# LSH attention and two MLP stages on one core: score pieces of 384 columns, another order of the attention, and one small addition moved to VectorE

## The chip, the cores and the metric

The kernel runs on one core of a Trainium2 chip. The metric is device time in microseconds of one execution. The core has TensorE (PE, matmuls, results in PSUM), VectorE (DVE), ScalarE (ACT), GpSimd (POOL) and SyncE (SP, which issues the DMAs); PEld in a profile is TensorE's loading of weights.

## The reference

The first part is attention over 2 batches and 8 heads, 768 positions of 64 dimensions. Queries and keys are hashed to 6 bits each, by the signs of their products with a random projection; a query attends only to the keys of its own bucket:

```python
mask = q_bucket[:, :, :, None] == k_bucket[:, :, None, :]
scores = scale * np.matmul(q, k.transpose(0, 1, 3, 2))
scores = np.where(mask, scores, -1000000000.0)
scores = scores - np.max(scores, axis=-1, keepdims=True)
attn = np.exp(scores)
attn = attn / (np.sum(attn, axis=-1, keepdims=True) + 1e-09)
return np.matmul(attn, v).astype(np.float32)
```

Its output, 1536 tokens of 512, goes through an MLP, `((x @ w1) * (x @ w2)) @ w3 @ w_out`, and that through a mixture of four experts, `out += p[e] * (relu(x @ e1[e]) @ e2[e])`.

## The kernel before

Every float32 matmul is made of products of parts: a value is split into a high part, rounded to the type that PE takes, and the low rest, and three of the four products are summed. Hence the many pairs "hi" (an ACT copy, or POOL's) and "lo" (a subtraction on DVE or POOL).

The attention works on 48 units (16 heads x 3 blocks of 256 queries). For each unit `unit(u)` records:

- S (two, of 128 queries each): the score matmuls into a tile `s_ps` of two PSUM banks, 768 key columns in the pieces `SEG` (512 and 256 columns). The sign bits of the hash ride along as extra rows (`kb`, `lo`), so that scores of other buckets become huge.
- mx (DVE, line 436): copies the score tile to `e` and takes its minimum per row (scores are negated).
- ex (ACT, line 439): the exponential in place, with the row sums in columns 6 and 7 of the small tile `sm`.
- r1 (POOL, line 452): adds 1e-9 to the two sums; r2 (DVE, line 454): the reciprocal of both.
- en (POOL, line 449, every fourth on ACT, line 448): normalizes `e` by it.
- T (PE, line 470): transposes of `e` into `t_ps`; hi (ACT, line 476) and lo (DVE, line 478) split them into `et`.
- pv (PE): products with the values into `pv_ps`; po (ACT, lines 496 and 503) and xa (DVE, line 498; from unit 27 on POOL, line 506, behind a DMA pm) sum the two halves into the MLP's input `xa`.

Per head, `head` records loads on the SP queue, splitting on POOL (lines 360, 167, 170) and copies by DMA; per two heads, `pair` records the sign bits: matmuls `bits_of`, in the same pieces `SEG`, the comparison `is_pos` on DVE (line 386) and DMA copies. `first_head` does it for head 0 alone, with the queries' comparison in two parts of 256 and 512 columns.

Beside the attention run the first 8 weight conversions (`conv64`, n from 0 to 7): each loads half a tile of 64-bit weights and turns it to high and low parts, with the DVE operations c0, c1, c2, c3 and cd (lines 207, 209, 212, 215, 220), two ACT operations and two POOL operations (lines 170 and 223). When `xa` of the first 512 tokens is there and their weights are converted, PE has 96 "fill" matmuls (fm) of the first MLP stage for times when it has no attention work (into `t_ps[2]`, which is free for them from unit 38 on, and `s_ps`). The rest of the MLP (`u_ps`, `o_ps`) begins when all attention work has ended.

The order of the work on all engines is written out by a planner, `emit_all`. Each operation is recorded by `op` with an engine, a duration in ns (fixed by hand), what it depends on, and a priority: its time T in units of P = 5500 plus P times the `RANK` of its group. The planner goes through the recorded durations, and on each engine takes the ready operation of the lowest priority value; the instructions are then issued in that order on each engine's queue. The ranks of the eight conversions are `C0 + n * CP`. So a changed duration or rank changes the order on every engine, PE and SP included, while what is computed stays.

Of the kernel before, what the change touches and what calls it, by code (L numbers as in the profile page):

```python
# [14 lines left out]
ALU = mybir.AluOpType  # L15
# [9 lines left out]
RANK = {
    "C0": 16.68,
    "CP": 16.1,
    "S0": -239.52,
    "S1": 27.05,
    "T0": -88.98,  # L30
    "T1": -71.39,
    "T2": -86.81,
    "b0": -70.87,
    "b1": -163.79,
    "bits": -188.45,
    "en": -138.6,
    "ex0": 12.29,
    "ex1": -50.98,
    "fd": -30.85,
    "fx": -49.15,  # L40
    "hi0": -17.87,
    "hi1": -151.69,
    "hi2": -87.16,
    "ld": -138.95,
    "lo0": -71.6,
    "lo1": -482.92,
    "lo2": -138.58,
    "lv": -106.52,
    "mx0": -542.16,
    "mx1": -84.39,  # L50
    "p0": -19.19,
    "p1": -131.31,
    "pm": -135.95,
    "po": -194.17,
    "pr2": -131.6,
    "prep": 2.16,
    "pv": 12.21,
    "r1": -72.77,
    "r2": -255.45,
    "v": 13.17,  # L60
    "xa": -226.06,
    "xb": -108.68,
}
GROUP = {
    **dict.fromkeys(("sc", "h", "l", "k1", "k2", "k3", "dq"), "prep"),
# [9 lines left out]
def tile_lsh_attention_moe(ctx, tc, qk, v, projc, w1, w2, w3T, w_out, dp, e1, e2, out):  # L75
    nc = tc.nc
    B, H, D2, S = qk.shape
# [33 lines left out]
    xa = const.tile([128, TT, DM], F32, name="xa")  # L111
# [6 lines left out]
    PC = projc.shape[1] - 1  # L118
# [3 lines left out]
    XP = 27  # L122
# [22 lines left out]
    sm_t = tiles(6, [128, 8], "sm")  # L145
    ap.tile([128, APAD], F32, name="apad")
    s_ps = tiles(2, [128, 1024], "s_ps", p=pp)
    SEG = (slice(0, 512), slice(512, S))
    pv_ps = pp.tile([128, 512], F32, name="pv_ps")[:, 0:256]
    t_ps = tiles(3, [128, 512], "t_ps", p=pp)  # L150
    f_ps = t_ps[2]
# [2 lines left out]
    def mm(o, l, r, start, stop):  # L154
        nc.tensor.matmul(out=o, lhsT=l, rhs=r, start=start, stop=stop)  # L155
# [30 lines left out]
    def conv64(n, dst, half, src):  # L186
        r = raws[n % NRAW]

        def hi_():
            return slots[dst][:, 0, half * 512:(half + 1) * 512]  # L190

        def lo_():
            return slots[dst][:, 1, half * 512:(half + 1) * 512]

        ri = r.bitcast(I32)
        lw, hw = (ri.rearrange("p (a b) -> p a b", b=2)[:, :, i] for i in range(2))
        c, t = cbuf[:, n % NCB, 0], cbuf[:, n % NCB, 1]
# [27 lines left out]

    P = 5500.0
# [21 lines left out]
    def op(key, eng, dur, fn, deps, prio, group=None):  # L248
        keys[key] = len(ops)
        group = group or group_of(key)  # L250
        ops.append((eng, dur, fn, deps, prio + P * RANK.get(group, 0.0), group))
# [122 lines left out]
        op(("vl", hh), "POOL", 956, lambda: pool_lo(vv[:, :, D:2 * D], rv, vv[:, :, 0:D]), [("vh", hh)], Tv)  # L374

    def bits_of(ps, hs):
        for r in SEG:
            for i, hh in enumerate(hs):
                a = hh % 2
                hi, lo = hh_t[hh % HR], ll_t[hh % HR]  # L380
                mm(ps[:, r], pbh[:, a, :], hi[:, r], i == 0, False)
                mm(ps[:, r], pbl[:, a, :], hi[:, r], False, False)
                mm(ps[:, r], pbh[:, a, :], lo[:, r], False, i == len(hs) - 1)

    def is_pos(dst, ps, r, c=slice(0, S)):
        nc.vector.tensor_scalar(out=dst, in0=ps[r, c], scalar1=thr[r], scalar2=amp[r], op0=ALU.is_gt, op1=ALU.mult)  # L386

    def first_head():
        ps, free_, n = take_s()
        lo, kb = ll_t[0], kb_t[0]  # L390
        q, k = slice(0, PC), slice(64, 64 + PC)
        T = -1e6
        op(("bm", -1), "PE", 970, lambda: bits_of(ps, (0,)), [("h", 0), ("l", 0), ("pb", 0)] + free_, T, "b0")
        op(("mk", 0), "DVE", 930, lambda: is_pos(kb[k], ps, k), [("bm", -1)], T, "b0")
        for i, (key, c) in enumerate(((("mq", 0), slice(0, 256)), (("sf", n), slice(256, S)))):
            op(key, "DVE", (330, 600)[i], lambda c=c: is_pos(lo[64:64 + PC, c], ps, q, c), [("mk", 0)], T + i, "b0")

    def pair(p):
        T = (2 * p - 1.6) * 3 * P
# [14 lines left out]
    def unit(u):  # L414
# [30 lines left out]
        def norm(t):  # L445
# [698 lines left out]
```

## Time and profile before

| | |
|---|---|
| median of 3 runs | 983.35 us (982.66 to 983.57) |
| the profiled execution, from first to last instruction (span) | 980.4 us; the page gives no other time of it |
| instructions | 14358 |
| PE busy | 966.2 us, 99% |
| PEld busy | 833.1 us, 85% |
| DVE busy | 718.6 us, 73% |
| ACT busy | 455.8 us, 46% |
| POOL busy | 200.4 us, 20%, all of it in the first 264 us |
| TensorE's granted clock | 1.00 throughout |

Busy shares are means over the whole span. The attention lies in about the first 264 us, the MLP stages behind it; the shares of the two parts differ much, so the views by stretch are the ones to read. A PE that counts as busy is not PE at its peak, since matmuls are pipelined and their ends are modelled. A time in brackets after an instruction is idle time of its engine ahead of it, with what ended it.

### The profile page before, as it was taken

How to read it: one execution, taken by the hardware profiler on the slowest of the kernel's cores; microseconds unless marked ns; L12 is line 12 of the kernel's file. 1: busy time of each engine (PE TensorE's matmuls, PEld its weight loads, DVE VectorE, ACT ScalarE, POOL GpSimd, SP SyncE). 2: the span in 40 equal slices, each digit the busy share in tenths (PEclk: the TensorE clock that was granted, in tenths of full speed). 3: DMA queues.
4: the chain of work that ended last, by engine and by line, in shares of the span. 5: the costliest groups of instructions: out<-in, count | busy, mean ns of one | idle time of the engine just before them, and what ended most of it. 6: DMA issues, size and time to landing. Idle time of an engine off the chain costs nothing.

```text
span 980.4 us, 14358 instructions
## 1 busy us (share of the span) xinstructions
PE 966.2 (99%) x5227; PEld 833.1 (85%) x5227; DVE 718.6 (73%) x1401; ACT 455.8 (46%) x864; POOL 200.4 (20%) x244
## 2 busy tenths in 40 slices
PE   8999999999999999999999999999999999999998
PEld 7999989888888888888888888888888888888886
DVE  7999999998599974964798745777457674476543
ACT  6999999987443422444543223322232322323121
POOL 6978878886100000000000000000000000000000
PEclk9999999999999999999999999999999999999999
DMA  6645444330133331330021102001021000200011
GB/s 171 184 124 137 114 105 116 90 92 12 54 126 113 127 108 43 110 106 1 22 65 44 44 1 84 25 22 35 9 75 34 22 24 21 64 22 1 1 65 66
DMA packets 42728, 65.58 MB, mean 67 GB/s; under 512 B 5752, under 2 KB 25784, under 8 KB 42656
## 3 DMA queue, kind: packets, MB, share of 16 engines
q1 hardware_dynamic: 42512, 64.65, 22.3%
q8 instruction: 41, 0.67, 0.3%
q14 instruction: 31, 0.25, 0.1%
q10 hardware_dynamic: 144, 0.01, 0.0%
HBM read 47.22 MB, written 3.15 MB: 51 GB/s over the span
## 4 chain that ended last, share of the span: by engine, by line
PE 86%; DVE 9%; POOL 2%; issue 1%; ACT 1%; DMA 0%; DVEq 0%; POOLq 0%; ACTq 0%
PE u_ps L155 50%; PE o_ps L155 22%; PE s_ps L155 5%; PE pv_ps L155 4%; PE t_ps L470 4%; DVE et L478 3%; DVE e L436 3%; PE t_ps L155 1%; PE t_ps L534 1%; DVE cbuf L215 0%; POOL e L449 0%; DVE xa L498 0%; DVE bt L386 0%; DVE cbuf L207 0%; ACT et L476 0%
## 5 line engine op out<-in xcount | busy, mean ns | idle before, releaser
L155 PE MATMUL o_ps<-slotl,hl 128*128 128x512 f32 x768 | 180.0, 390 | 0.0
L155 PEld LDWEIGHTS o_ps<-slotl,hl 128*128 128x128 f32 x768 | 142.9, 188 | 28.9
L155 PE MATMUL u_ps<-xh,slotl 128*128 128x512 f32 (+1 forms) x672 | 137.2, 359 | 0.0
L155 PEld LDWEIGHTS u_ps<-xh,slotl 128*128 128x128 f32 x672 | 114.3, 189 | 18.7
L155 PE MATMUL u_ps<-xh,slot 128*128 128x512 f32 (+1 forms) x576 | 116.8, 353 | 0.0
L155 PEld LDWEIGHTS u_ps<-xh,slot 128*128 128x128 f32 x576 | 97.8, 189 | 16.6
L951 DVE TENSOR_TENSOR m<-m,u_ps 128x512 f32<-128x512 f32 x96 | 63.2, 682 | 62.1 <-PE u_ps L155 60.8
L478 DVE TENSOR_TENSOR et<-t_ps,et 128x512 fp32r<-128x512 f32 x144 | 96.4, 680 | 4.8 <-ACT et L476 4.3
L439 ACT ACTIVATE e<-e,sm 128x768 f32<-128x768 f32 x96 | 89.8, 938 | 10.4 <-DVE e L436 9.7
L436 DVE TENSOR_SCALAR_CACHE_REDUCE e<-s_ps 128x768 f32<-128x768 f32 x96 | 90.4, 945 | 2.1 <-PE t_ps L470 1.0
L155 PE MATMUL pv_ps<-et,vv 128*128 128x256 f32 x576 | 89.3, 294 | 0.9 <-DVE xa L498 0.4
L470 PE MATMUL t_ps<-ident,e 128*128 128x128 f32 x576 | 84.2, 274 | 4.3 <-DVE et L478 3.9
L155 PE MATMUL u_ps<-slotl,hl 128*128 128x512 f32 x384 | 87.7, 389 | 0.0
L476 ACT ACTIVATE et<-t_ps 128x512 fp32r<-128x512 f32 x144 | 82.1, 595 | 9.9 <-PE t_ps L470 5.8
L155 PEld LDWEIGHTS u_ps<-slotl,hl 128*128 128x128 f32 x384 | 72.1, 188 | 15.0
L470 PEld LDWEIGHTS t_ps<-ident,e 128*128 128x128 f32 x576 | 66.0, 140 | 13.2 <-DVE et L478 5.6
L155 PEld LDWEIGHTS pv_ps<-et,vv 128*128 128x128 f32 x576 | 74.3, 190 | 2.0 <-DVE xa L498 0.6
L449 POOL TENSOR_SCALAR e<-e,sm 128x768 f32<-128x768 f32 x72 | 65.9, 922 | 8.1 <-DVE sm L454 5.7
L946 DVE SCALAR_TENSOR_TENSOR hl<-gl,hl 128x512 fp32r<-128x512 f32 x32 | 22.1, 692 | 47.7 <-ACT hl L1088 47.7
L943 ACT ACTIVATE hl<-m 128x512 fp32r<-128x512 f32 x32 | 20.3, 633 | 76.6 <-DVE m L951 76.6
L161 ACT ACTIVATE m<-u_ps 128x512 f32<-128x512 f32 x32 | 19.1, 598 | 79.0 <-issue 61.9
L155 PE MATMUL s_ps<-ka,hh 128*128 128x512 f32 x192 | 52.8, 356 | 3.1 <-DVE e L436 2.5
(157 smaller groups left out, 1563.0 us busy)
## 6 DMA issues: line engine op xcount, KB each, us to landing
wraw<-in_e SPq DMA_DIRECT2D x64, 256.0 KB
wraw<-in_w SPq DMA_DIRECT2D x16, 512.0 KB
wraw<-in_w3T SPq DMA_DIRECT2D x16, 512.0 KB
r<-in_qk SPq DMA_DIRECT2D x15, 384.0 KB
wraw<-in_w_out SPq DMA_DIRECT2D x8, 512.0 KB
rv<-in_v SPq DMA_DIRECT2D x16, 192.0 KB
ka<-hh SPq DMA_DIRECT2D x15, 192.0 KB
kb<-hh SPq DMA_DIRECT2D x15, 192.0 KB
```

Source lines behind the costliest of these rows:

```text
L155: nc.tensor.matmul(out=o, lhsT=l, rhs=r, start=start, stop=stop)
L161: nc.scalar.activation(out=dst, in_=ps, func=AF.Copy)
L436: op(("mx", u, t), "DVE", 873, lambda ps=ps, m=m, e=e: nc.vector.tensor_scalar(out=e, in0=ps[:, 0:S], scalar1=THR, scalar2=None, op0=ALU.m ...
L439: op(("ex", u, t), "ACT", 921, lambda e=e, m=m, rs=rs: nc.scalar.activation(out=e, in_=e, func=AF.Exp, scale=-1.0, bias=m, accum_out=rs), ...
L449: return "POOL", 872, lambda: nc.gpsimd.tensor_scalar(out=e, in0=e, scalar1=r[:, t:t + 1], scalar2=1.0, op0=ALU.mult, op1=ALU.mult)
L470: nc.tensor.transpose(out=ps[:, k, t * 128:(t + 1) * 128], in_=e_t[2 * (u % ER) + t][:, kt * 128:(kt + 1) * 128], identity=ident)
L476: op(("hi", n), "ACT", 480, lambda ps=ps, et=et: nc.scalar.activation(out=et[:, 0], in_=ps, func=AF.Copy), [("T", u, j), ("pv", n - NET)], Tj)
L478: op(("lo", n), "DVE", 602, lambda ps=ps, et=et: nc.vector.tensor_tensor(out=et[:, 1], in0=ps, in1=f(et[:, 0]), op=ALU.subtract), [("hi", ...
L534: nc.tensor.transpose(out=t_ps[i % 2][:, 0:128], in_=ident, identity=ident)
L943: op(key, "ACT", 480, lambda: nc.scalar.activation(out=hl_t[n % 2][:, 0], in_=m_t[m], func=AF.Relu), after, clock[0])
L946: op(key, "DVE", 602, lambda: nc.vector.scalar_tensor_tensor(out=hl_t[n % 2][:, 1], in0=src(), scalar=0.0, in1=f(hl_t[n % 2][:, 0]), op0=A ...
L951: nc.vector.tensor_tensor(out=out, in0=a, in1=b, op=o)
```

## The change

Four things are done.

- `SEG` now holds pairs of a place in PSUM and a range of columns: the score tile's 768 columns lie as 384 in the first 512 of the tile and 384 in the second 512. Score and sign matmuls are 384 columns each. `row` and `cols` let DVE read such a tile as two runs of 384. The first head's comparison is two parts of 384.
- r1 is recorded on DVE, as the same tensor_scalar on the same two columns, with 75 ns in place of 295 for the planner.
- The planner's durations for the first eight conversions' DVE operations, for S and for pv are other numbers.
- `RANK` is another table, and each of the eight conversions has a rank of its own (cv0 to cv7) in place of `C0 + n * CP`.

```diff
-    SEG = (slice(0, 512), slice(512, S))
+    SEG = ((slice(0, 384), slice(0, 384)), (slice(512, 896), slice(384, S)))
+
+    def row(ps, r=slice(0, 128)):
+        return ps[r].rearrange("p (a b) -> p a b", a=2)[:, :, 0:384]
+
+    def cols(x):
+        return x.rearrange("p (a b) -> p a b", a=2)
...
-        slow = (400, 700, 2700) if beside else (335, 602, 1460)
+        slow = (616, 750, 2700, 365, 792) if beside else (335, 602, 1460, 335, 335)
...
-            ("DVE", slow[0], [("c0", n)], "c1",
+            ("DVE", slow[3], [("c0", n)], "c1",
...
-            ("DVE", slow[0], [("c2", n)], "c3",
+            ("DVE", slow[4], [("c2", n)], "c3",
...
-        for i, (key, c) in enumerate(((("mq", 0), slice(0, 256)), (("sf", n), slice(256, S)))):
-            op(key, "DVE", (330, 600)[i], lambda c=c: is_pos(lo[64:64 + PC, c], ps, q, c), [("mk", 0)], T + i, "b0")
+        for i, (key, c) in enumerate(((("mq", 0), SEG[0]), (("sf", n), SEG[1]))):
+            op(key, "DVE", 470, lambda c=c: is_pos(lo[64:64 + PC], ps, q, c), [("mk", 0)], T + i, "b0")
...
-                for c in SEG:
-                    mm(ps[:, c], hi[:, r], ka[:, c], True, False)
-                for c in SEG:
-                    mm(ps[:, c], lo[0:64 + PC, r], kb[0:64 + PC, c], False, True)
+                for w, c in SEG:
+                    mm(ps[:, w], hi[:, r], ka[:, c], True, False)
+                for w, c in SEG:
+                    mm(ps[:, w], lo[0:64 + PC, r], kb[0:64 + PC, c], False, True)
...
-                out=e, in0=ps[:, 0:S], scalar1=THR, scalar2=None, op0=ALU.min,
+                out=cols(e), in0=row(ps), scalar1=THR, scalar2=None, op0=ALU.min,
...
-        op(("r1", u), "POOL", 295, lambda: nc.gpsimd.tensor_scalar(
+        op(("r1", u), "DVE", 75, lambda: nc.vector.tensor_scalar(
             out=sm[:, 0:2], in0=sm[:, 6:8], scalar1=1e-9, scalar2=None, op0=ALU.add), ex, T + 2 * P)
...
-                t = (RANK["C0"] + n * RANK["CP"]) * P if T is None else T
                 hold = [("ex", CR[0] + CR[1] * n, 0)] if T is None and key == "cl" else []
-                op((key, n), eng, dur, go, deps + after + hold, t - (1.5 * P if key == "cl" else 0))
+                op((key, n), eng, dur, go, deps + after + hold, (T or 0) - (1.5 * P if key == "cl" else 0),
+                   f"cv{n}" if T is None else None)
```

Of the rank table, some lines (the groups of S, mx, ex, r1, r2 and pv):

```diff
-    "S0": -239.52,
-    "S1": 27.05,
+    "S0": -910.56,
+    "S1": -133.30,
...
-    "ex0": 12.29,
-    "ex1": -50.98,
+    "ex0": -42.65,
+    "ex1": -277.42,
...
-    "mx0": -542.16,
-    "mx1": -84.39,
+    "mx0": -945.19,
+    "mx1": -868.68,
...
-    "pv": 12.21,
-    "r1": -72.77,
-    "r2": -255.45,
+    "pv": -299.11,
+    "r1": -952.53,
+    "r2": -1188.22,
```

## Rows read from the trace of the kernel before

**Rows 1.** Windows: length, busy PE, PEld, DVE, ACT, POOL; clock, DMA, GB/s.
```profile
20.00:50.00 30.00, 29.75 (x218) 27.93 (x219) 27.65 (x60) 27.41 (x56) 27.41 (x34) 1.00 0.74 198
50.00:100.00 50.00, 49.35 (x363) 45.49 (x363) 49.43 (x106) 48.16 (x96) 40.15 (x48) 1.00 0.47 124
100.00:150.00 50.00, 49.05 (x358) 44.76 (x356) 49.54 (x104) 46.97 (x94) 40.90 (x49) 1.00 0.44 111
150.00:200.00 50.00, 47.95 (x352) 44.37 (x351) 49.87 (x101) 46.43 (x97) 43.08 (x53) 1.00 0.38 102
200.00:230.00 30.00, 27.30 (x188) 23.89 (x186) 29.82 (x56) 23.20 (x47) 24.30 (x27) 1.00 0.24 67
230.00:264.00 34.00, 34.00 (x216) 30.19 (x215) 18.29 (x34) 22.42 (x45) 12.39 (x17) 1.00 0.14 44
```

**Rows 2.** Chain of waits, 116 to 150 us: shares; start, us, what.
```profile
by line: DVE et L478 35.2%; DVE e L436 29.6%; DVE xa L498 7.5%; issue 5.9%; DVE cbuf L215 4.9%; DVE bt L386 2.9%; DVE cbuf L212 2.6%; PE t_ps L470 1.9%; DVE sm L454 1.9%; DVE psum_t L541 1.9%; DVE cbuf L220 1.8%; ACT et L476 1.8%; DVE cbuf 
...
131.01 0.17 DVE sm L454
```

**Rows 3.** Instructions in time, 236 to 264 us: start, us, what, [idle before].
```profile
241.95 0.69 DVE L478 TENSOR_TENSOR et<-t_ps,et 128x512 fp32r<-128x512 f32 x1 [0.59 <-ACT et L476]
...
253.09 0.69 DVE L478 TENSOR_TENSOR et<-t_ps,et 128x512 fp32r<-128x512 f32 x1 [0.55 <-ACT et L476]
...
256.46 2.89 PE L155 MATMUL t_ps<-xh,slot 128*128 128x512 f32 x12
257.24 0.73 POOL L506 TENSOR_TENSOR xa<-pvs,pvd 64x256 f32<-64x256 f32 x1 [1.36 <-DMA pvd<-pvs]
...
263.26 1.07 PE L155 MATMUL u_ps<-xh,slot 128*128 128x512 f32 x4
```

**Rows 4.** Groups of POOL, 0 to 264 us: busy us, mean ns | idle before, releasers.
```profile
L452 POOL TENSOR_SCALAR sm<-sm 128x2 f32<-128x2 f32 x48 | 14.3, 297 | 20.7 <-ACT e L439 17.1 <-DMA ka<-hh 0.5
```

**Rows 5.** Groups of DVE by shape, 0 to 264 us.
```profile
L436 DVE TENSOR_SCALAR_CACHE_REDUCE e<-s_ps 128x768 f32<-128x768 f32 x96 | 90.4, 945 | 2.1 <-PE t_ps L470 1.0 <-PE s_ps L155 0.8
...
L454 DVE RECIPROCAL sm<-sm 128x2 f32<-128x2 f32 x48 | 7.5, 156 | 2.7 <-POOL sm L452 2.3
...
L215 DVE TENSOR_SCALAR cbuf<-cbuf 128x512 int32<-128x512 int32 x8 | 7.2, 898 | 0.0
L207 DVE TENSOR_SCALAR cbuf<-cbuf 128x512 f32<-128x512 f32 x8 | 6.6, 829 | 0.0
...
L209 DVE TENSOR_SCALAR cbuf<-cbuf 128x512 int32<-128x512 int32 x8 | 3.8, 472 | 0.0
```

**Rows 6.** Groups of DVE by shape, 264 to 430 us.
```profile
L215 DVE TENSOR_SCALAR cbuf<-cbuf 128x512 int32<-128x512 int32 x32 | 13.6, 425 | 0.8
L209 DVE TENSOR_SCALAR cbuf<-cbuf 128x512 int32<-128x512 int32 x32 | 13.5, 422 | 0.4
L207 DVE TENSOR_SCALAR cbuf<-cbuf 128x512 f32<-128x512 f32 x32 | 13.4, 420 | 0.3 <-ACT cbuf L205 0.3
```

**Rows 7.** Instructions in order of time, 124 to 127 us.
```profile
124.19 1.01 POOL L170 TENSOR_TENSOR vv<-rv,vv 128x384 fp32r<-128x384 f32 x1
...
124.61 0.62 DVE L541 TENSOR_SCALAR psum_t<-psum_t 128x12 f32<-128x12 f32 x1
...
125.27 0.23 DVE L542 RECIPROCAL psum_t<-psum_t 128x12 f32<-128x12 f32 x1
```

**Rows 8.** Groups of PE by shape, 0 to 400 us: score matmuls.
```profile
L155 PE MATMUL s_ps<-kb,ll 76*128 76x512 f32 x96 | 38.1, 397 | 0.0
L155 PE MATMUL s_ps<-kb,ll 76*128 76x256 f32 x96 | 26.9, 281 | 0.0
```

**Rows 9.** Groups of DVE, 0 to 264 us: first head's comparison.
```profile
L386 DVE TENSOR_SCALAR ll<-s_ps,thr,amp 12x512 fp32r<-12x512 f32 x1 | 0.8, 792 | 0.0
...
L386 DVE TENSOR_SCALAR ll<-s_ps,thr,amp 12x256 fp32r<-12x256 f32 x1 | 0.5, 534 | 0.0
```

**Rows 10.** Groups of PE by shape, 0 to 400 us: fill matmuls.
```profile
L155 PE MATMUL t_ps<-xh,slot 128*128 128x512 f32 x84 | 23.5, 399 | 0.0
```

More of the change, by code (lines that the diff above doesn't have):

```diff
@@ L25 @@
 RANK = {
-    "C0": 16.68,
-    "CP": 16.1,
-    "S0": -239.52,
-    "S1": 27.05,
[L30 to L36, printed above, removed]
-    "ex0": 12.29,
-    "ex1": -50.98,
[L39 to L48, printed above, removed]
-    "mx0": -542.16,
-    "mx1": -84.39,
[L51 to L56, printed above, removed]
-    "pv": 12.21,
-    "r1": -72.77,
-    "r2": -255.45,
-    "v": 13.17,
-    "xa": -226.06,
-    "xb": -108.68,
+    "S0": -910.56,
+    "S1": -133.30,
+    "T0": -888.79,
+    "T1": -931.07,
+    "T2": -879.52,
+    "b0": -865.54,
+    "b1": -906.91,
+    "bits": -432.45,
+    "cv0": -150.25,
+    "cv1": -532.18,
+    "cv2": -284.36,
+    "cv3": -432.05,
+    "cv4": -852.82,
+    "cv5": -595.40,
+    "cv6": -388.77,
+    "cv7": -50.88,
+    "en": -854.64,
+    "ex0": -42.65,
+    "ex1": -277.42,
+    "fd": -861.09,
+    "fx": -596.11,
+    "hi0": -903.22,
+    "hi1": -946.67,
+    "hi2": -866.08,
+    "ld": -331.77,
+    "lo0": -867.03,
+    "lo1": -933.55,
+    "lo2": -867.06,
+    "lv": -270.73,
+    "mx0": -945.19,
+    "mx1": -868.68,
+    "p0": -869.22,
+    "p1": -1118.00,
+    "pm": -1100.93,
+    "po": -1009.27,
+    "pr2": -905.76,
+    "prep": -429.80,
+    "pv": -299.11,
+    "r1": -952.53,
+    "r2": -1188.22,
+    "v": -39.72,
+    "xa": -866.61,
+    "xb": -902.16,
 }
@@ L376, in bits_of @@
     def bits_of(ps, hs):
-        for r in SEG:
+        for w, r in SEG:
             for i, hh in enumerate(hs):
@@ L380, in bits_of, with is_pos @@
                 hi, lo = hh_t[hh % HR], ll_t[hh % HR]
[L381 to L386, printed above, removed]
+                mm(ps[:, w], pbh[:, a, :], hi[:, r], i == 0, False)
+                mm(ps[:, w], pbl[:, a, :], hi[:, r], False, False)
+                mm(ps[:, w], pbh[:, a, :], lo[:, r], False, i == len(hs) - 1)
+    def is_pos(dst, ps, r, c=None):
+        src, dst = (row(ps, r), cols(dst)) if c is None else (ps[r, c[0]], dst[:, c[1]])
+        nc.vector.tensor_scalar(out=dst, in0=src, scalar1=thr[r], scalar2=amp[r], op0=ALU.is_gt, op1=ALU.mult)
     def first_head():
@@ L426, in score @@
                 r = slice(qp * 256 + t * 128, qp * 256 + (t + 1) * 128)
-                for c in SEG:
-                    mm(ps[:, c], hi[:, r], ka[:, c], True, False)
-                for c in SEG:
-                    mm(ps[:, c], lo[0:64 + PC, r], kb[0:64 + PC, c], False, True)
+                for w, c in SEG:
+                    mm(ps[:, w], hi[:, r], ka[:, c], True, False)
+                for w, c in SEG:
+                    mm(ps[:, w], lo[0:64 + PC, r], kb[0:64 + PC, c], False, True)
             m, rs = (sm[:, 2 * i + t:2 * i + t + 1] for i in (0, 3))
             Tt = T + t * P / 2
-            op(("S", u, t), "PE", 690, score, [(k, hh) for k in ("mq", "mk", "k1", "k2", "k3", "dq")] +
+            op(("S", u, t), "PE", 694, score, [(k, hh) for k in ("mq", "mk", "k1", "k2", "k3", "dq")] +
                ([("sf", 0)] if 0 < u < NQ else []) + free_, Tt)
             op(("mx", u, t), "DVE", 873, lambda ps=ps, m=m, e=e: nc.vector.tensor_scalar(
-                out=e, in0=ps[:, 0:S], scalar1=THR, scalar2=None, op0=ALU.min,
+                out=cols(e), in0=row(ps), scalar1=THR, scalar2=None, op0=ALU.min,
                 op1=ALU.min, accum_out=m), [("S", u, t), ("en", u - 6, 0), ("en", u - 6, 1)] + [("T", u - ER, j) for j in range(3)], Tt)
@@ L492, in unit @@
             n = NJ * u + j
-            op(("pv", n), "PE", 472, lambda j=j: pv(j), [("lo", n), ("vl", hh), ("xa" if u - 1 < XP else "po", u - 1), ("pv", n - 1)], Tp)
+            op(("pv", n), "PE", 480, lambda j=j: pv(j), [("lo", n), ("vl", hh), ("xa" if u - 1 < XP else "po", u - 1), ("pv", n - 1)], Tp)
         a, t0 = slice((h % 2) * D, (h % 2 + 1) * D), b * S + qp * 256
```

## The prediction

> **What bounds the kernel now.** The table of windows comes first. Up to about 264 us the attention runs, after it the two MLP stages, in which TensorE has no idle time worth the name and which the change leaves as they are: all that the change can win or lose lies in the first 264 us. There the reader is to see two engines near their limit at once. VectorE (DVE) is busy 49.43, 49.54 and 49.87 of 50 us in the three windows from 50 to 200, and 29.82 of 30 after that; TensorE (PE) is busy 49.35, 49.05 and 47.95, a little less. From 230 on it turns round: PE is full, DVE is busy 18.29 of 34 us. GpSimd (POOL) has 10, 9 and 7 us free in each 50. [rows 1] The chain of waits says the same for the middle: from 116 to 150 us it runs along DVE, 35.2% in the subtraction of line 478 and 29.6% in the minimum of line 436. [rows 2] So in the middle an added DVE microsecond is a microsecond, and one taken from POOL or from PE's wait for POOL is worth nothing. The end needs one more view, the instructions in order of time. DVE's last attention operation begins at 253.09, POOL's last sum into xa ends at 257.24 + 0.73 = 257.97, and the MLP's first matmul follows only at 263.26, after fill matmuls that PE still had to do. [rows 3] The attention chain thus ends 5.3 us before PE is through: so much delay of DVE is free.
>
> **r1 moves from POOL to DVE.** This is the part that costs. It is 48 instructions of 128x2. On POOL they take 0.297 us each, 14.3 us together, and POOL stood 20.7 us idle ahead of them. [rows 4] POOL is no bound, so I give nothing for its relief; what it gives to DVE is the 2.3 us that the reciprocal waited for r1. [rows 5]
>
> On DVE the nearest row for the bare instruction is the reciprocal on the same two columns, 0.156 us, and the chain counts it 0.17 where it lies on the path. [rows 2, 5] 48 x 0.15 = 7.2 us.
>
> But r1 is a tensor_scalar from SBUF to SBUF, and this form behaves differently while POOL works. The conversion's tensor_scalars (lines 207, 209, 215) take 0.829, 0.472 and 0.898 us in the attention, and 0.420, 0.422 and 0.425 us after 264 us, where POOL has stopped. [rows 5, 6] The excess is 0.41, 0.05 and 0.47 us, 0.31 on the mean of the 24. One instance shows what it is. Line 541, of 128x12 only, takes 0.62 us from 124.61 to 125.23; POOL runs one instruction from 124.19 to 125.20; the reciprocal that follows at 125.27 takes 0.23. [rows 7] The small tensor_scalar sat there until POOL was done, and r1 differs from it by having 2 columns in place of 12.
>
> [...]
>
> So the wait of one r1 lies between 0 and 0.47 us on the mean. I take 0.31. Against the upper end speaks that POOL is idle for 17.1 us of the attention just when it awaits the exponentials that r1 awaits too [rows 4]: in some units r1 will find POOL standing still. Against zero speaks that POOL is busy over 80% of the windows from 50 to 200 [rows 1], and still over three quarters without r1's own 0.3 us in each unit of some 5. 48 x 0.31 = 14.9 us, and with the bare instruction 22.1 us. Behind a waiting r1 in DVE's queue stand the minimum of the next scores, the subtractions and r2; for these wait ACT's exponentials, PE's value products and transposes, and POOL's and ACT's normalization. That is DVE's whole load, so nothing hides the wait.
>
> **Scores in two pieces of 384.** A score tile has 4 matmuls over 512 + 256 columns and then 4 over 384 + 384: as many columns, matmuls and weight loads. By duration the pieces are 397 and 281 ns [rows 8], half-way 339, so 4 x 339 against 2 x (397 + 281): zero. Bounds: if a piece of 384 cost as much as one of 512, 96 x 2 x 0.116 = 22 us on PE at the worst; if as much as 256, the same as a gain; the straight line between is what I take, the sizes being evenly spaced. The sign matmuls (96) go with it. The minimum reads the same 768 columns, now from two banks with a step between them: 945 ns as before. The nearest other row is the comparison in two parts, 534 and 792 ns for 256 and 512 columns [rows 9], a fixed part near 0.28 us per instruction; here the instruction is not split, so at the worst it costs that, 96 x 0.28 = 27 us, and at the best it saves nothing. I take zero. The first head's comparison becomes two of 384: the first score waits for one of about 0.66 in place of 0.53, 0.13 us once at the start.
>
> **Order set anew.** DVE's work doesn't shrink by it. What it can reach: the 3.7 us that DVE is idle between 20 and 230 us [rows 1], DVE's eight waits from 241 to 254, 4.9 us together [rows 3], and the fill matmuls, 84 into t_ps and 12 into s_ps [rows 10]; twelve in a row take 2.89 us [rows 3], so all of them 23 us, and put earlier than the end they would fill PE's gaps of the middle. It moves the weight conversions too, with their loads on the SP queue among the head loads and the copies of signs, and their DVE operations among the minima: a load that is put ahead of a copy the scores await would hold PE. Bounds: a gain of 5.3 us (below that the attention chain itself is late) and a loss of as much again. I take zero for the choice of order by itself; that a late DVE no longer has to wait for others is taken into the sum.
>
> **Sum.** 22.1 - 2.3 = 19.8 us more on DVE. Off go the 5.3 us free at the end, about 3 of the 4.9 us of waits from 241 to 254 (PE and ACT are ahead of a late DVE), and 2.5 us of the 3.7 in the middle: 19.8 - 5.3 - 3 - 2.5 = +9.0 us. The profiled span is 980.4 us, 3 us below the median of the runs, 983.35, which is what lies around it; the change falls into the span alone. 983.35 + 9 = 992.4, so **992 us**.
>
> **Rivals.** (1) Faster: r1 mostly finds POOL standing still, and the new order closes the tail. r1 then costs 7.2 - 2.3 = 4.9 us of DVE, the eight waits give as much back, and the fill matmuls lie in PE's gaps; the end moves up to the chain's, 5.3 us less, less 1 for the first units: 979 us. For it: POOL's 20.7 us of waits ahead of r1, at the same moment of a unit [rows 4]. Against it: POOL no longer has r1 in its queue to stop it there, and fills that time with head preparation or a conversion, 0.9 to 1.8 us each. The place is DVE's queue at r1; the sign turns where the mean wait is below about (5.3 + 5.5 + 2.3) / 48 - 0.15 = 0.12 us. (2) No change: r1 costs a little, and the free time at the end swallows it: 983 us. For it, the 5.3 us [rows 3]; against it, that it needs a wait near that same 0.12 us. (3) Much slower: r1 takes the full 0.47, the reciprocal behind it cannot overlap with it (line 542's 0.23 in place of 0.15 [rows 7]), and none of the gaps absorbs anything but the 5.3: 48 x 0.70 - 2.3 - 5.3 = +26, 1009 us. For it, lines 207 and 215; against it, line 209, which waits 0.05.
>
> **Chances.** Forecast 0.50, with its own range 985 to 1001; rival 1 0.27; rival 2 0.11; rival 3 0.12. Order and score pieces with their open bounds are why rival 1 holds as much as it does. The range reaches to rival 1's centre and a third of the way into rival 3: 978 to 1003 leaves out about 0.10 below and 0.08 above. 0.2% is 2 us, about what a measurement of this kernel can tell from no change: faster 0.27, same 0.11, slower 0.62.
>
> **What would show it.** In the changed kernel's groups: the row of r1 on DVE with a mean near 0.45 us (rival 1 if near 0.2); score matmuls of 384 columns near 339 ns; the minimum at 945 ns; DVE over 98% busy from 50 to beyond 200 us; the MLP's first matmul at about 272 us in place of 263.26, and everything after it as long as before. The prediction is wrong in its mechanism if r1 stays at the reciprocal's duration, or if its wait is there and the MLP begins no later.

## The result, and the profile after

The changed kernel takes 991.15 us (median of 6 runs, 989.41 to 994.21), the kernel before 982.85 beside it (982.24 to 983.57): a ratio of 1.0088, 95% interval 1.0079 to 1.0098, or +8.3 us. 992 us was forecast. The profiled execution is the slowest of the six (994.21 us; span 991.9 against 980.4), so its differences are some 3 us larger than those of the medians.

Windows of the changed kernel (length; busy PE, PEld, DVE, ACT, POOL; clock, DMA, GB/s), to set beside [rows 1]:

```profile
20.00:50.00 30.00, 28.20 (x195) 26.59 (x194) 26.09 (x60) 24.88 (x48) 19.68 (x20) 0.94 0.72 188
50.00:100.00 50.00, 48.92 (x344) 44.91 (x344) 49.69 (x110) 45.86 (x93) 38.82 (x39) 1.00 0.44 117
100.00:150.00 50.00, 47.92 (x335) 43.33 (x334) 49.57 (x106) 45.03 (x90) 35.41 (x36) 1.00 0.39 95
150.00:200.00 50.00, 48.08 (x344) 46.24 (x343) 48.83 (x105) 43.66 (x89) 38.16 (x40) 0.97 0.43 111
200.00:230.00 30.00, 29.71 (x210) 27.93 (x209) 30.00 (x64) 26.83 (x55) 21.75 (x23) 1.00 0.28 81
230.00:264.00 34.00, 32.58 (x225) 29.41 (x224) 33.24 (x67) 26.53 (x54) 20.98 (x22) 1.00 0.10 30
```

DVE is nearly full from 50 to 264 us now (48.83 of 50 us at the least), where before it had nearly half of 230 to 264 free. POOL, rid of r1, is emptier up to 230 us. PE is less full in four of the six windows, and its clock, 1.00 in all of [rows 1], falls in two (0.94 and 0.97; more on that at the end).

Groups of DVE, 0 to 275 us, beside [rows 5]:

```profile
L450 DVE TENSOR_SCALAR_CACHE_REDUCE e<-s_ps 128x768 f32<-128x768 f32 x96 | 90.2, 944 | 3.7 <-PE t_ps L484 2.3 <-PE s_ps L168 1.3
L466 DVE TENSOR_SCALAR sm<-sm 128x2 f32<-128x2 f32 x48 | 21.9, 456 | 1.2 <-ACT e L453 1.1
...
L468 DVE RECIPROCAL sm<-sm 128x2 f32<-128x2 f32 x48 | 7.4, 153 | 0.3
```

r1 (line 466) is there with 0.456 us on the mean, 21.9 us in all; the reciprocal behind it and the minimum are as before. One r1 in order of time, as [rows 7] showed it of line 541:

```profile
83.93 1.29 POOL L183 TENSOR_TENSOR xh<-xa,xh 128x512 fp32r<-128x512 f32 x1
...
84.44 0.80 DVE L466 TENSOR_SCALAR sm<-sm 128x2 f32<-128x2 f32 x1
...
85.72 0.17 DVE L468 RECIPROCAL sm<-sm 128x2 f32<-128x2 f32 x1
```

POOL's instruction ends at 83.93 + 1.29 = 85.22, r1 at 84.44 + 0.80 = 85.24. The shortest r1 takes 0.148 us, the median one 0.199, the longest 1.927: 23 of the 48 take at most 0.17 us and meet no wait, and each of the other 25 ends 0.02 to 0.03 us after an instruction of POOL's.

The end of the attention, beside [rows 3]:

```profile
262.41 1.19 PE L168 MATMUL pv_ps<-et,vv 128*128 128x256 f32 x8
...
264.37 0.63 PE L168 MATMUL pv_ps<-et,vv 128*128 128x256 f32 x4
...
264.84 2.02 PE L168 MATMUL t_ps<-xh,slot 128*128 128x512 f32 x8
...
266.69 1.30 PE L168 MATMUL s_ps<-xh,slot 128*128 128x512 f32 x5
...
267.48 0.73 POOL L520 TENSOR_TENSOR xa<-pvs,pvd 64x256 f32<-64x256 f32 x1 [1.01 <-ACT g L174]
...
267.83 2.88 PE L168 MATMUL t_ps<-xh,slot 128*128 128x512 f32 x12
...
270.55 1.52 PE L168 MATMUL s_ps<-xh,slot 128*128 128x512 f32 x6
...
271.91 2.88 PE L168 MATMUL t_ps<-xh,slot 128*128 128x512 f32 x12
...
274.63 0.62 PE L168 MATMUL u_ps<-xh,slot 128*128 128x512 f32 x2
```

POOL's last sum ends at 267.48 + 0.73 = 268.21 (257.97 before), the MLP begins at 274.63 (263.26 before), behind 8 + 5 + 12 + 6 + 12 = 43 fill matmuls that follow the last value products (264.37). From there to the end the two kernels take 717.3 and 717.1 us.

The difference is thus all in the attention, as forecast. The experiments below divide the 8.3 us so: r1 as a bare instruction on DVE +4.8, its wait for POOL +12.2, the new order -8.7, the pieces of 384 nothing. This is the division along one path, with r1 moved in the old order first. In the new order the same wait costs 10.7 us, and with an r1 that doesn't wait, or none, the new order is worth 7.2 and 6.7 us.

### The profile page after: what moved, and what is told of

The parts are those of the page before. It is cut to its first block, busy times and chain, and to the rows that moved or that the text cites. A ratio compares the mean times of both kernels' runs of the same rounds, so it can differ in the third digit from the quotient of the medians.

```text
span 991.9 us, 14406 instructions
## 1 busy us (share of the span) xinstructions
PE 972.9 (98%) x5227; PEld 842.3 (85%) x5227; DVE 733.9 (74%) x1449; ACT 456.1 (46%) x864; POOL 187.9 (19%) x196
## 3 DMA queue, kind: packets, MB, share of 16 engines
q1 hardware_dynamic: 42512, 64.65, 22.1%
## 4 chain that ended last, share of the span: by engine, by line
PE 80%; DVE 15%; issue 2%; ACT 1%; POOL 1%; DMA 1%; DVEq 0%; SPq 0%; POOLq 0%; ACTq 0%
PE u_ps L168 50%; PE o_ps L168 22%; DVE et L492 5%; DVE e L450 4%; PE s_ps L168 3%; PE pv_ps L168 3%; PE t_ps L484 2%; DVE sm L466 2%; PE t_ps L168 1%; DVE cbuf L228 1%; DVE xa L512 1%; DVE bt L400 0%; ACT e L453 0%; DMA r<-in_qk 0%; POOL e L463 0%
## 5 line engine op out<-in xcount | busy, mean ns | idle before, releaser
L168 PEld LDWEIGHTS u_ps<-xh,slot 128*128 128x128 f32 x576 | 97.8, 189 | 16.5
L168 PE MATMUL pv_ps<-et,vv 128*128 128x256 f32 x576 | 92.5, 299 | 1.0 <-DVE et L492 1.0
L168 PEld LDWEIGHTS pv_ps<-et,vv 128*128 128x128 f32 x576 | 77.0, 195 | 3.0 <-DVE et L492 1.2
L484 PEld LDWEIGHTS t_ps<-ident,e 128*128 128x128 f32 x576 | 67.1, 141 | 12.2 <-DVE et L492 5.0
L168 PE MATMUL s_ps<-ka,hh 128*128 128x384 f32 x192 | 53.3, 359 | 6.0 <-DVE e L450 4.0
L960 DVE SCALAR_TENSOR_TENSOR hl<-gl,hl 128x512 fp32r<-128x512 f32 x32 | 22.1, 692 | 47.7 <-ACT hl L1102 47.7
```

The lines of the kernel that those rows point to most:

```text
L484: nc.tensor.transpose(out=ps[:, k, t * 128:(t + 1) * 128], in_=e_t[2 * (u % ER) + t][:, kt * 128:(kt + 1) * 128], identity=ident)
L960: op(key, "DVE", 602, lambda: nc.vector.scalar_tensor_tensor(out=hl_t[n % 2][:, 1], in0=src(), scalar=0.0, in1=f(hl_t[n % 2][:, 0]), op0=A ...
```

## The experiments

Theory W: r1's wait for POOL's running instruction is the cost. Its rivals: the new order is slow by itself (O), any added DVE instruction costs as much (B), or a wait of DVE's queue for the exponentials (Q). In all runs the order of the instructions was kept as the kernel in question has it, unless the text says otherwise. The kernel before, run beside them, took 982.68, 982.83 and 982.53 us in the three sets; the ratios are to it.

**A reciprocal in r1's place, in the changed kernel.**

```diff
-        op(("r1", u), "DVE", 75, lambda: nc.vector.tensor_scalar(
-            out=sm[:, 0:2], in0=sm[:, 6:8], scalar1=1e-9, scalar2=None, op0=ALU.add), ex, T + 2 * P)
+        op(("r1", u), "DVE", 75, lambda: nc.vector.reciprocal(
+            out=sm[:, 0:2], in_=sm[:, 6:8]), ex, T + 2 * P)
```

> The changed kernel with r1 on DVE at the same place, but as a reciprocal of the same two columns (so the divisors come out inverted twice and the normalization is wrong). Theory W (r1 waits for POOL's running instruction): in the changed kernel r1 takes 0.456 us on the mean and the reciprocal behind it 0.153; as a reciprocal it should take 0.15 to 0.16, so DVE sheds 48 x 0.30 = 14.5 us, and of the 8.3 us between the kernels most goes: 983 to 986 us. Theory O (the new order itself is slow: PE runs empty between 12 and 50 us, weight conversions on DVE among the minima): within 2 us of the changed kernel, 989 to 993, though r1 is short. Theory B (one more instruction in DVE's queue is what costs, whatever its kind): 988 to 991.

980.41 us, ratio 0.9976 (0.9968 to 0.9985): 10.7 us less than the changed kernel, and even 2.3 less than the kernel before. Groups of DVE in its attention:

```profile
L468 DVE RECIPROCAL sm<-sm 128x2 f32<-128x2 f32 x48 | 7.5, 156 | 0.3
L466 DVE RECIPROCAL sm<-sm 128x2 f32<-128x2 f32 x48 | 7.4, 155 | 1.2 <-ACT e L453 1.1
```

Same place, same columns, same number of instructions: 0.155 in place of 0.456 us. B and O fall: an instruction that doesn't wait costs little, and the order is not slow but fast. W had the direction; it went further than it said.

**No r1, in the changed kernel.**

```diff
-        op(("r1", u), "DVE", 75, lambda: nc.vector.tensor_scalar(
-            out=sm[:, 0:2], in0=sm[:, 6:8], scalar1=1e-9, scalar2=None, op0=ALU.add), ex, T + 2 * P)
-        op(("r2", u), "DVE", 81, lambda: nc.vector.reciprocal(out=sm[:, 2:4], in_=sm[:, 0:2]), [("r1", u)], T + 2 * P)
+        op(("r1", u), "DVE", 75, lambda: None, ex, T + 2 * P)
+        op(("r2", u), "DVE", 81, lambda: nc.vector.reciprocal(out=sm[:, 2:4], in_=sm[:, 6:8]), [("r1", u)], T + 2 * P)
```

> The changed kernel in the same order without r1: the reciprocal reads the sums themselves (1e-9 is left out; a row sum is at least 1, its own largest term, so in float32 the addition changes nothing). Theory W: DVE sheds all 21.9 us of r1, 7.4 us more than with the reciprocal in its place; the end then lies at PE's or the tail's bound: 979 to 983 us. Theory O: 988 to 992.

977.05 us, ratio 0.9946 (0.9934 to 0.9959): lower than W had it, and the version that beats both kernels. Chains of waits from 100 to 150 us, shares by line, first of the changed kernel, then of this one:

```profile
by line: DVE et L492 30.0%; DVE e L450 27.6%; issue 9.0%; DVE sm L466 7.2%; DVE xa L512 5.9%; PE s_ps L168 4.6%; DVE cbuf L228 3.3%; PE pv_ps L168 3.2%; PE t_ps L484 2.3%; DVE sm L468 2.0%; DVE bt L400 2.0%; DVE cbuf L225 1.2%; ACT et L490 
```

```profile
by line: PE s_ps L168 38.2%; PE pv_ps L168 28.4%; PE t_ps L483 25.3%; DVE et L491 3.8%; DVE e L450 1.8%; issue 1.8%; DVE cbuf L222 1.0%
```

With r1 the chain runs along DVE, r1 itself holding 7.2% of it; without, the three shares of PE make 92%. DVE no longer sets the pace there.

**r1 back on POOL, in the changed kernel.** The plan still has it on DVE, so the order is the new one.

```diff
-        op(("r1", u), "DVE", 75, lambda: nc.vector.tensor_scalar(
+        op(("r1", u), "DVE", 75, lambda: nc.gpsimd.tensor_scalar(
```

> The changed kernel with the instructions of all engines in the order that its planner wrote, but r1 issued on POOL at that place of the order. Theory W: DVE sheds 21.9 us, POOL takes 48 x 0.3 = 14 us back of its 80 us of idle time, and the reciprocal waits now and then for POOL: 980 to 985 us. Theory O: 988 to 993.

986.04 us, ratio 1.0036 (1.0023 to 1.0049): above what W gave. DVE sheds r1, but the reciprocal now waits for POOL:

```profile
L468 DVE RECIPROCAL sm<-sm 128x2 f32<-128x2 f32 x48 | 7.7, 160 | 10.7 <-POOL sm L466 9.8
```

9.8 us in place of the 2.3 of [rows 5]: 11 times in all DVE's queue comes to the reciprocal before POOL is done with r1, and DVE stands. The new order is made for an r1 that isn't on POOL.

**r1 on DVE, in the kernel before.**

```diff
-        op(("r1", u), "POOL", 295, lambda: nc.gpsimd.tensor_scalar(
+        op(("r1", u), "POOL", 295, lambda: nc.vector.tensor_scalar(
```

> The kernel before in its own order (planned with r1 on POOL), only r1 issued on DVE at its place of that order. Theory W: r1 near 0.45 us on the mean with waits behind POOL, DVE +20 us, of which the end's free time and other gaps take a part: +6 to +13 us, 989 to 996. Theory O: the old order is the good one, +0 to +3 us, 983 to 986.

999.88 us, ratio 1.0175 (1.0161 to 1.0188): +17.2 us, more than W had it. This is the part "r1 moves" by itself. Its r1, in a group of DVE:

```profile
L452 DVE TENSOR_SCALAR sm<-sm 128x2 f32<-128x2 f32 x48 | 23.3, 486 | 0.5 <-ACT e L439 0.5
```

What DVE had to do up to its last subtraction into `et`, in the kernel before and in this one (a window each; the third number after the length is DVE's busy time):

```profile
0.00:253.78 253.78, 244.00 (x1728) 222.54 (x1729) 237.51 (x490) 222.11 (x438) 198.88 (x242) 1.00 0.42 111
```

```profile
0.00:270.76 270.76, 249.26 (x1728) 222.42 (x1729) 257.30 (x538) 224.29 (x438) 186.99 (x194) 1.00 0.40 104
```

DVE is busy 19.8 us longer (less than the 23.3 of r1, since the records of neighbours overlap, in the changed kernel's trace by up to 0.10 us before or behind an r1), and its idle time falls from 16.3 to 13.5 us only: the last subtraction ends 17.0 us later. Where the free time at the end stayed, the end of this kernel shows:

```profile
271.11 0.63 PE L155 MATMUL pv_ps<-et,vv 128*128 128x256 f32 x4
...
271.58 0.86 PE L155 MATMUL t_ps<-xh,slot 128*128 128x512 f32 x3
...
272.29 1.31 PE L155 MATMUL s_ps<-xh,slot 128*128 128x512 f32 x5
...
273.44 2.89 PE L155 MATMUL t_ps<-xh,slot 128*128 128x512 f32 x12
274.23 0.73 POOL L506 TENSOR_TENSOR xa<-pvs,pvd 64x256 f32<-64x256 f32 x1 [1.99 <-DMA pvd<-pvs]
...
276.17 1.52 PE L155 MATMUL s_ps<-xh,slot 128*128 128x512 f32 x6
...
277.52 2.88 PE L155 MATMUL t_ps<-xh,slot 128*128 128x512 f32 x12
...
280.25 1.98 PE L155 MATMUL u_ps<-xh,slot 128*128 128x512 f32 x8
```

POOL's last sum ends at 274.96, the MLP begins at 280.25: again 5.3 us. Behind the last value products (271.11) PE has 3 + 5 + 12 + 6 + 12 = 38 fill matmuls, and it comes to them, in its queue's fixed order, only then. In the kernel before the same 38 follow its last value products:

```profile
254.13 0.63 PE L155 MATMUL pv_ps<-et,vv 128*128 128x256 f32 x4
```

Both they and the MLP come 17.0 us later here: a late DVE moves them along.

**A reciprocal on DVE in r1's place, in the kernel before.**

```diff
-        op(("r1", u), "POOL", 295, lambda: nc.gpsimd.tensor_scalar(
-            out=sm[:, 0:2], in0=sm[:, 6:8], scalar1=1e-9, scalar2=None, op0=ALU.add), ex, T + 2 * P)
+        op(("r1", u), "POOL", 295, lambda: nc.vector.reciprocal(
+            out=sm[:, 0:2], in_=sm[:, 6:8]), ex, T + 2 * P)
```

> The kernel before in its own order, with r1 issued on DVE as a reciprocal of the same two columns (divisors inverted twice, the normalization is wrong). As the addition on DVE it took 999.88 us, r1 0.486 us on the mean. Theory W (the wait for POOL): r1 falls to 0.156 us, DVE sheds 48 x 0.33 = 15.8 us, nearly all of which came through: 984 to 987 us. Theory Q (an r1 placed for POOL's queue makes DVE's queue wait for the exponentials): the time stays above 993 us.

987.65 us, ratio 1.0044 (1.0032 to 1.0057), r1 0.154 us; Q falls. The wait costs 999.88 - 987.65 = 12.2 us of the 48 x 0.33 = 15.8, the bare instruction 987.65 - 982.83 = 4.8 of 7.4 us (W's range missed by 0.65 us).

**No r1, in the kernel before** (the plan keeps its 295 ns).

```diff
-        op(("r1", u), "POOL", 295, lambda: nc.gpsimd.tensor_scalar(
-            out=sm[:, 0:2], in0=sm[:, 6:8], scalar1=1e-9, scalar2=None, op0=ALU.add), ex, T + 2 * P)
-        op(("r2", u), "DVE", 81, lambda: nc.vector.reciprocal(out=sm[:, 2:4], in_=sm[:, 0:2]), [("r1", u)], T + 2 * P)
+        op(("r1", u), "POOL", 295, lambda: None, ex, T + 2 * P)
+        op(("r2", u), "DVE", 81, lambda: nc.vector.reciprocal(out=sm[:, 2:4], in_=sm[:, 6:8]), [("r1", u)], T + 2 * P)
```

> The kernel before in its own order without r1: the reciprocal reads the sums themselves (1e-9 left out, which changes nothing in float32 at sums of at least 1). It shows what r1 cost where it was, on POOL. If POOL's relief is worth nothing but the 2.3 us that the reciprocal waited for it, as the prediction had it: 980.5 to 983 us. If the hand-over from ACT over POOL to DVE lay on the path in most units: 976 to 979. The distance to the changed kernel without r1 (977.05) is then what the order and the pieces of 384 give.

983.79 us, ratio 1.0011 (1.0002 to 1.0020), a little above the first of the two ranges: POOL's r1 cost nothing where it was, and taking it off gains nothing. So the 5.6 us by which the changed kernel without r1 beats the kernel before are not r1's; 983.79 - 977.05 = 6.7 us are the order's.

**The pieces of 384 alone, in the kernel before** (`row`, `cols` and all uses as in the change, durations and ranks as before).

```diff
-    SEG = (slice(0, 512), slice(512, S))
+    SEG = ((slice(0, 384), slice(0, 384)), (slice(512, 896), slice(384, S)))
```

> The kernel before with the score and sign matmuls, the minimum and the comparisons in two pieces of 384, and nothing else. Theory Z (as many columns, no difference): 982.2 to 983.4 us; score matmuls of 384 near 339 ns and the minimum near 945 ns. Theory P (the pieces are what makes the changed kernel without waits 2.3 us faster): 980 to 981 us.

982.94 us, ratio 1.0002 (0.9993 to 1.0011): Z. Groups of its PE and of its DVE, the score matmuls and the minimum:

```profile
L162 PE MATMUL s_ps<-kb,ll 76*128 76x384 f32 x192 | 49.6, 339 | 0.0
```

```profile
L444 DVE TENSOR_SCALAR_CACHE_REDUCE e<-s_ps 128x768 f32<-128x768 f32 x96 | 90.4, 945 | 1.7 <-PE s_ps L162 0.8 <-PE t_ps L478 0.7
```

339 ns, half-way between the 397 and 281 of [rows 8], and 945 ns as in [rows 5].

**The changed kernel without r1 in the plan either.**

```diff
-        op(("r1", u), "DVE", 75, lambda: nc.vector.tensor_scalar(
-            out=sm[:, 0:2], in0=sm[:, 6:8], scalar1=1e-9, scalar2=None, op0=ALU.add), ex, T + 2 * P)
-        op(("r2", u), "DVE", 81, lambda: nc.vector.reciprocal(out=sm[:, 2:4], in_=sm[:, 0:2]), [("r1", u)], T + 2 * P)
+        op(("r2", u), "DVE", 81, lambda: nc.vector.reciprocal(out=sm[:, 2:4], in_=sm[:, 6:8]), ex, T + 2 * P)
```

> The changed kernel without r1 in the plan too, so that the planner's order is free to move again (in the run before, r1's 75 ns still stood in the plan). If the rank table suits the order as such: within 1.5 us of 977.05. If its gain hangs on the very order for which it was written: 979 to 983 us.

986.91 us, ratio 1.0047 (1.0034 to 1.0059), outside both ranges: with the same instructions and ranks as the run of 977.05, 9.9 us more. In the profiles its last value products end 5.0 us later (254.66 against 249.68), and 56 fill matmuls in place of 43 stand behind them. 75 ns less in the plan reshuffle the order, and the table of ranks is worth its gain only with the durations for which it was written.

**r1 in the form that also accumulates, in the changed kernel.** Theory F, of this run and the next: r1's wait hangs on the form of the instruction, not on the addition or its columns.

```diff
         op(("r1", u), "DVE", 75, lambda: nc.vector.tensor_scalar(
-            out=sm[:, 0:2], in0=sm[:, 6:8], scalar1=1e-9, scalar2=None, op0=ALU.add), ex, T + 2 * P)
+            out=sm[:, 0:2], in0=sm[:, 6:8], scalar1=1e-9, scalar2=None, op0=ALU.add,
+            op1=ALU.min, accum_out=sm[:, 4:5]), ex, T + 2 * P)
```

> The changed kernel, r1 the same addition on DVE, but in the form of tensor_scalar that also gives out an accumulated value (the form of the minimum), into an unused column. [...] Theory A (any addition from SBUF to SBUF of these columns waits): 989 to 993 us.

**r1 with two inputs from SBUF, in the changed kernel** (`eps` is a 128x2 tile filled with 1e-9 at the start; the unused tile behind it is two columns smaller; both are left out here).

```diff
-        op(("r1", u), "DVE", 75, lambda: nc.vector.tensor_scalar(
-            out=sm[:, 0:2], in0=sm[:, 6:8], scalar1=1e-9, scalar2=None, op0=ALU.add), ex, T + 2 * P)
+        op(("r1", u), "DVE", 75, lambda: nc.vector.tensor_tensor(
+            out=sm[:, 0:2], in0=sm[:, 6:8], in1=eps, op=ALU.add), ex, T + 2 * P)
```

> The changed kernel, r1 the same addition on DVE, but with 1e-9 read from a second small SBUF tile (tensor_tensor). In the kernel before the tensor_tensor of two SBUF inputs at line 164 took 0.958 us beside POOL and 0.684 after 264 us. Theory F by that row: two inputs from SBUF wait for POOL too, with r1 at 0.40 to 0.46 us: 988 to 993 us. Theory G (only the tensor_scalar form waits, the row of line 164 has another reason): r1 near 0.16 us, 980 to 982 us.

980.18 us (ratio 0.9980, 0.9971 to 0.9989) and 989.72 us (1.0079, 1.0065 to 1.0093): F in both (A had at least 989 for the first), though r1 with two inputs waits a little less than F had it (0.372 us against 0.40 to 0.46). Their r1, in the same groups:

```profile
L466 DVE TENSOR_SCALAR_CACHE_REDUCE sm<-sm 128x2 f32<-128x2 f32 x48 | 6.9, 145 | 1.4 <-ACT e L453 1.3
```

```profile
L467 DVE TENSOR_TENSOR sm<-sm,eps 128x2 f32<-128x2 f32 x48 | 17.9, 372 | 1.2 <-ACT e L454 1.1
```

The same addition of the same columns at the same place takes 0.145 us in the accumulating form, 0.372 with two inputs from SBUF, and 0.456 in the plain form of the changed kernel. The first is no longer than the reciprocal in its place (0.155 us), the other two are longer by 0.22 and 0.30 us on the mean. So the plain form waits on two columns too, as line 541 did on twelve. What it is in a form that makes it wait, no run shows.

**Holes of PE filled, in the changed kernel without r1.** `pv_full` is the PSUM tile of which `pv_ps` is the first 256 columns; the lines stand at the end of `score`.

```diff
+                for _ in range({(0, 1): 7, (2, 0): 4, (2, 1): 9}.get((u, t), 0)):
+                    nc.tensor.transpose(out=pv_full[:, 256:384], in_=ident, identity=ident)
```

> The changed kernel without r1 (977.05 us), with 20 transposes of the identity into unused PSUM columns put behind the scores of units 0 (second tile: 7) and 2 (4 and 9), where PE stood idle 0.89, 0.48 and 1.06 us; nothing else moves. In the new order the granted clock falls to 0.5 for some 3 us from about 19 us on, after these holes; in the order before it stays at 1.00. Theory C (the holes bring the clock down and the slow stretch delays the first units): granted clock 1.00 from 12 to 30 us and 0.7 to 2.5 us less: 974.5 to 976.4 us. Theory D (DVE sets the pace from 50 us on and swallows what PE wins before): within 0.6 us of 977.05.

976.96 us, ratio 0.9944 (0.9932 to 0.9957): D by the medians. Windows of the run without r1, then of this one:

```profile
16.00:18.00 2.00, 1.30 (x6) 0.67 (x5) 1.89 (x5) 1.42 (x4) 2.00 (x3) 1.00 0.74 180
18.00:20.00 2.00, 1.16 (x8) 1.16 (x9) 0.90 (x3) 1.87 (x5) 2.00 (x3) 0.83 0.38 78
20.00:22.00 2.00, 2.00 (x9) 2.00 (x9) 1.44 (x3) 1.64 (x4) 2.00 (x2) 0.50 0.93 203
22.00:24.00 2.00, 2.00 (x13) 2.00 (x13) 1.33 (x3) 1.05 (x2) 2.00 (x3) 0.82 1.01 231
```

```profile
18.00:20.00 2.00, 1.95 (x18) 1.68 (x16) 1.07 (x5) 1.80 (x3) 2.00 (x4) 1.00 0.22 45
20.00:22.00 2.00, 2.00 (x16) 2.00 (x14) 1.40 (x4) 2.00 (x6) 2.00 (x2) 1.00 0.84 186
22.00:24.00 2.00, 2.00 (x15) 1.86 (x15) 2.00 (x5) 1.56 (x3) 2.00 (x3) 1.00 0.98 207
```

The clock stays at 1.00 here, and the medians differ by 0.1 us only. But they hardly test Theory C, since by the mean clock the fall does not come in every execution. Without the fill three of the five executions have a mean clock of 0.999 or 1.000 and take 976.77 to 977.05 us; the other two, of which one was profiled, have 0.998 and 0.997 and take 978.26 and 978.09. With the fill all five have 0.999 or 1.000 and take 976.48 to 977.09. In the profiles the MLP begins at 258.06 us in place of 259.31. So where the clock falls, the time is some 1.2 us longer, within what Theory C gave it; five executions each are too few to show that the fill always keeps the clock up.

## Why the prediction was right, and where it was not

- **r1's wait.** 0.31 us on the mean was forecast from 24 other tensor_scalars; it is 0.456 - 0.155 = 0.30. The wait is shown from three sides: by the ends that fall together (25 r1 end 0.02 to 0.03 us after an instruction of POOL's), by three other forms of r1 at the same place (0.155, 0.145 and 0.372 us), and in both orders (0.456 and 0.486 us). That the size was met so closely is in part luck: 0.31 is the mean of excesses as different as 0.41, 0.05 and 0.47 us, and nearly half of the 48 r1 don't wait at all.
- **The bare instruction.** 7.2 us was forecast, and the 48 records sum to 7.4. But records of neighbours overlap: with the reciprocal in the kernel before, DVE's busy time up to its last subtraction into `et` grows by 4.9 us (237.5 to 242.4), and 4.8 arrive at the end.
- **What the gaps absorb.** This step failed. The forecast took 13.1 us off r1's 22.1: 2.3 that the reciprocal had waited, and 10.8 of other gaps. In the kernel before with r1 on DVE, DVE's busy time grew by 19.8 us and its idle time fell by 2.8; 999.88 - 982.68 = 17.2 arrived, where +9.0 was forecast. "5.3 us free at the end" are not free: PE reaches the 38 fill matmuls in its queue only behind the last value products, so they move along with a late DVE.
- **"I take zero for the choice of order by itself".** This failed too. The new order is worth 991.15 - 999.88 = -8.7 us with r1 as it is, 980.41 - 987.65 = -7.2 with a reciprocal in its place, 977.05 - 983.79 = -6.7 without. The bound of 5.3 us on the gain took the end of the attention chain as fixed, and "DVE's work doesn't shrink" by the order does not hold: without r1 in both orders DVE's last subtraction into `et` ends at 248.69 us in place of 255.11, with 233.6 us of DVE's work ahead of it in place of 238.6 (one subtraction into `xh` now comes behind it).
- **The sum.** The two errors, 8.2 us too little for r1 and 8.7 us of order left out, cancel by luck, which is why 992 meets 991.15: the parts of the sum are better judged by the experiments than by its total.
- **Pieces and POOL.** Zero for both was right (982.94 and 983.79 against 982.83). But of the 2.3 us that the reciprocal had waited for r1 nothing shows at the end when r1 is taken off POOL: DVE's idle time up to its last subtraction stays as it was, 16.5 us against 16.3.
- **The rivals.** Rival 1 needed an r1 without waits; where it got one, by another form, the kernel is indeed faster than before, 980.2 to 980.4 us against the 979 it was given. Its way there was another: it had the fill matmuls in PE's gaps, and in the new order 43 of them stand behind the last value products where 38 stood before.
- **The signs.** r1's mean, the minimum's 0.944 us, pieces near 339 ns, a late MLP (274.63 in the profiled execution, the slowest) and the same time behind it came as said. DVE is over 98% busy in all windows from 50 to 230 us but one (48.83 of 50 from 150 to 200).

What in the new order makes the 7 us stays open. It lies ahead of the last value products: the five more fill matmuls behind them take 1.1 us back. Without r1 PE holds most of the chain from 100 to 150 us in both orders, 92% in the new one, as shown above, and 69% in the old:

```profile
by line: PE s_ps L155 27.8%; PE t_ps L469 20.7%; PE pv_ps L155 20.4%; DVE e L436 10.6%; DVE et L477 10.5%; issue 4.8%; DVE xa L497 2.2%; DVE cbuf L220 1.2%; DVE psum_t L540 0.7%; DVE sm L453 0.6%; DVE psum_t L541 0.5%; DVE cbuf L207 0.3%; D
```

PE's idle time from 50 to 200 us falls from 4.3 to 0.9 us between these two runs, DVE's idle time ahead of the subtractions into `et` from 5.2 to 2.8, and the conversions' five DVE operations from 34.0 to 30.4. The conversions can't be all of it: with a reciprocal as r1 they take 32.0 and 31.7 us, and the new order is worth 7.2 us all the same. Which of the ranks does it was not tried, since each change of the plan moves the whole order.

## What to carry to other kernels

Before a small instruction goes to DVE, look at its form, not its size: a plain tensor_scalar from SBUF to SBUF waited in 25 of 48 cases until POOL's running instruction had ended (0.30 us on the mean of all, 1.8 at the most, on two columns), and a reciprocal or the accumulating form of the same addition did not (0.155 and 0.145 us on the mean). Where engines work through their queues in a fixed order, time that seems free at the end of a stage is no cushion if other work (here the 38 fill matmuls in PE's queue, which came 17.0 us later with DVE's last subtraction) stands behind the instructions that wait for the late engine. And the cheapest r1 is none: sums that are at least 1 don't change by 1e-9 in float32, and without the addition the changed kernel takes 977.05 us in the order that was planned with it (986.91 when planned anew).

## What was not expected

Windows of the kernel before, then of the changed kernel, where the first units run:

```profile
16.00:18.00 2.00, 1.55 (x10) 1.11 (x9) 1.86 (x3) 1.41 (x4) 2.00 (x3) 1.00 0.74 164
18.00:20.00 2.00, 1.71 (x14) 1.27 (x11) 1.60 (x4) 2.00 (x5) 1.83 (x4) 1.00 0.27 49
20.00:22.00 2.00, 1.81 (x11) 1.64 (x12) 1.78 (x4) 1.29 (x3) 2.00 (x3) 1.00 0.92 295
```

```profile
20.00:25.00 5.00, 3.33 (x22) 2.69 (x21) 3.87 (x10) 4.25 (x8) 4.68 (x5) 0.96 0.70 151
25.00:30.00 5.00, 5.00 (x30) 4.90 (x31) 2.71 (x6) 3.32 (x7) 1.94 (x3) 0.70 0.89 259
190.00:200.00 10.00, 8.98 (x57) 8.95 (x58) 8.89 (x21) 7.75 (x15) 5.70 (x8) 0.83 0.27 85
```

In the changed kernel the granted clock falls from 1.00 to 0.50 around 25 and again around 192 us (it is 0.50 in all of 25 to 28 and of 192 to 194; 0.70 and 0.83 are means over the windows), each time after a stretch in which PE had stood idle: it was busy 0.25 of the last 1 us before 25, and 0.32 of the 2 us before 191. The kernel before keeps 1.00 at its start, which has holes too, with PE busy 1.55 and 1.71 of 2 us from 16 to 20, against 1.30 and 1.16 in the run without r1, whose clock fell. The changed kernel's runs spread over 4.8 us, those of the kernel before over 1.3, and the time goes roughly with the mean clock: 989.41 us at 0.999, 989.72 and 991.43 at 0.998, 990.87 and 994.21 at 0.996, 993.10 at 0.995. With the reciprocal as r1 it is 979.45 to 979.48 us at 1.000 and 982.11 at 0.997. So a part of the 8.3 us, perhaps 1 to 2 us (an estimate from 991.15 and 989.41), goes with falls of the clock, which no term of the prediction had. That the clock makes the spread is likely, not shown; the difference between the kernels stays without it, since the changed kernel's fastest run is 6.6 us above the median of the kernel before.

Three r1 of the changed kernel (at 180.91, 204.27 and 212.47 us) took 0.154 to 0.158 us although POOL's record shows a normalization running. These three records are 1.10 to 1.34 us long, where the median one is 0.91; in each a conversion operation of DVE was running when the normalization began, and the record ends 0.78 us after that operation and 0.70 us after r1. So here POOL seems to have waited for DVE, and its record to hold the wait; that reading was not tested.
